# A new port rule in a kernel's scheduler, and its VectorE exponentials placed anew

## The chip, the cores and the metric

The kernel runs on one core of one Trainium2 chip. The metric is the device time of one execution in microseconds. A core has TensorE (PE, matrix products), ScalarE (ACT), VectorE (DVE), GpSimd (POOL) and SyncE (SP, which here only issues DMAs). Each engine runs its own instructions strictly in the order in which they were emitted, and waits for the others by semaphores.

## The reference

Two branches share one input of 2048 tokens by 640 features and are mixed by a gate. Branch A is a long convolution over the tokens, branch B is attention with 32 query heads of width 20 and one common key and value head.

```python
x = A_q
g = _sigmoid((x * gate_w).sum(-1, keepdims=True))
# A: short convolution of k (4 taps), times v, then a causal convolution of length 2048
kv = k_shift * v
y = irfft(rfft(pad(kv)) * rfft(pad(ssm_k)))[:S]
a = x * (y + kv * ssm_D)
# B: multi-query attention over all 2048 tokens, no mask
q, k, v = x @ wq, x @ wk, x @ wv
p = softmax(q k^T * 20 ** -0.5)
b = (p v) @ wo
out = g * a + (1 - g) * b
```

(The code is shortened; all inputs are bfloat16.) The exponentials of the softmax are the bulk: 32 x 2048 x 2048 of them.

## The kernel before

*The attention stream.* The work is cut into groups G of four heads by 512 queries, 32 in all (8 for each block of 512 queries). A group walks through 16 key blocks j of 128 keys. For each (G, j) there are four tiles, one for each head, of 128 keys by 512 queries. TensorE computes a tile's scores into a PSUM bank (`score`, L1205 in the profile), ScalarE takes the exponential (`EXP`, L1242), and TensorE multiplies the result with the values into the group's accumulator bank (`PVmm`, L1283). Tiles go to ScalarE in units of three and two by turns: a unit of three tiles is written to a buffer ETA (one instruction of 1536 columns), a unit of two to ETB (1024 columns). There are three buffers of each kind. PSUM banks 0 to 2 and 3 to 4 hold the scores of the A and the B unit, bank 6 is the accumulator, and banks 5 and 7 serve everything else. The last group is cut into three stages (`STAGES`), so that its end is short.

*Exponentials on VectorE.* The table `DVE_J` lists, for each group, the key blocks j of which two of the four tiles are not given to ScalarE. Such a (G, j) is called a pair here. `stream` takes the two tiles out of ScalarE's sequence and `DEXP` computes them: each tile's scores are made by a score matmul of their own in bank 5 or 7 (it "rides" beside the stream's score matmuls in other rows of the array), VectorE brings each to dW (L1272, 512 columns), and three `scalar_tensor_tensor` instructions on 1024 columns make the exponential (L1275, L1276, both writing dX, and L1278 writing ETd). The values' matmul of a pair is a floating one: it is put in when it is ready, and at the latest ahead of the group's last value matmul. There are two dW, one dX and four ETd.

*The end of a group.* `norm` copies the accumulator to SBUF (acc, VectorE, L1351), sends the denominators through DRAM by three DMAs (den, scr_d, rbc) with a reciprocal on VectorE between (L1356), and GpSimd multiplies (oTn or oT, L1363). A DMA carries the result to DRAM for the output projection of that block of queries (L1662 and L1665; for the last block part of it directly, L1388 and L1391).

*The convolution.* It runs beside the stream as spectral products: for five blocks of 128 channels, TensorE computes spectra of kv and of the filter (`spectra`, L1566), VectorE evicts them to X and K (L1579, L1585, L1587), GpSimd multiplies them (`mac`, L1599, tiles Pp and AB), and TensorE transforms back (`inverse`, L1632), with VectorE's eviction into kv (L1642). Its transform tables are made in the first 75 us, in part by GpSimd.

*What sets the order.* Nothing in the order is written out by hand. `build` makes a graph of operations with dependencies, priorities and an estimated cost each, and `Scheduler` simulates the five engines by these costs when the kernel is built. Whenever an engine is free in this plan, `pick` chooses an operation and `place` sets its start and end; the order in which operations are placed is the instruction order that `emit` writes out, together with the semaphore waits. A wrong cost thus changes no result, only the order. ScalarE's exponentials and TensorE's matmuls of the stream are a fixed main sequence; all else is fitted in around it. Where TensorE would be idle for long in the plan, filler matmuls that write nothing needed are put in (L1714).

*The port.* VectorE and GpSimd share a read port of SBUF. Operations that use it carry `port=True`: VectorE's three steps of a pair, the squares sq, table steps and a few more. In `place`, one variable `port_until` says until when the port is taken; a VectorE operation with the mark and every GpSimd operation begin no earlier than that and move it to their own end. `pool_may` further lets GpSimd start only when VectorE's last planned instruction doesn't use the port, or none is soon to.

Of the kernel before, what the change touches and what calls it, by code (L numbers as in the profile page):

```python
# [48 lines left out]
class Op:  # L49
# [4 lines left out]
    def __init__(self, eng, fn, cost, kind, name, prio):  # L54
        self.unit = None
        self.eng = eng
        self.fn = fn
        self.deps = set()
        self.cost = cost
        self.kind = kind  # L60
        self.name = name
        self.prio = prio
        self.grp = None
        self.alts = None
        self.port = False
        self.nbytes = 0
        self.main = False
        self.cont = False
        self.nun = 0
        self.succ = []  # L70
        self.ready = 0.0
        self.start = None
        self.end = None
        self.placed = False
        self.sig = False
        self.value = None
        self.lane = None
        self.known = None
        self.seq = -1
        self.banks = None  # L80
        self.last = False
        self.urge = False
        self.floating = False
        self.tail = ()
        self.attached = False
        self.lat = 2.2
        self.iss = 0.35
        self.row = None
        self.soft = ()
        self.cols = frozenset()  # L90
        self.hole = frozenset()
# [78 lines left out]
class Scheduler:  # L170


    def __init__(self, graph, bank_free=(0, 1, 2, 3, 4, 5, 6, 7)):
        self.g = graph
        self.order = {e: [] for e in ENGS}
        self.linear = []
        self.t = {e: BEGIN for e in ENGS}
        self.bank_ready = {b: 0.0 for b in range(8)}
        self.bank_last = {b: [] for b in range(8)}
        self.bank_busy = {b: False for b in range(8)}  # L180
        self.bank_claimed = {b: False for b in range(8)}
        self.port_until = 0.0
        self.dma_bw = 0.0
        self.lanes = [[] for _ in range(NLANES)]
        self.main_started = False
        self.filler = None
        self.acc = None
        self.can_fill = False
        self.filler0 = None
        self.float_left = []  # L190
        self.active = []
        self.rows = set()
        self.mode = "f"
# [255 lines left out]
    def place(self, op, e):  # L449
        t = self.t[e]  # L450
        op.eng = e
        if e == "pe":
            mode = MODE.get(op.name, "f")
            if mode != self.mode:
                t += SWITCH
                self.mode = mode
        if op.alts:
            for x in op.alts:
                self.cand[x].discard(op)
            op.fn, op.cost = op.alts[e]  # L460
        else:
            self.cand[e].discard(op)
        if op.main and e == "pe":
            for b in op.banks or ():
                if not self.bank_claimed[b]:
                    self.bank_claimed[b] = True
                    op.deps.update(self.bank_last[b])
        start = max(t, op.ready)
        if op.kind == "d":
            if op.nbytes:  # L470
                begin = max(start + 0.1, self.dma_bw)
                self.dma_bw = begin + op.nbytes / 300e3
                op.end = max(self.dma_bw, start + op.iss) + op.lat
            else:
                op.end = start + op.iss + op.lat
            self.t[e] = start + op.iss
            best = min(range(NLANES), key=lambda l: self.lanes[l][-1].end if self.lanes[l] else -1.0)
            op.lane = best
            if self.lanes[best]:
                op.deps.add(self.lanes[best][-1])  # L480
            self.lanes[best].append(op)
            op.value = 16 * len(self.lanes[best])
        else:
            if (op.port and e == "dve") or e == "pool":
                start2 = max(start, self.port_until)
                op.end = start2 + op.cost
                self.port_until = op.end
            else:
                op.end = start + op.cost
            self.t[e] = op.end  # L490
        op.start = start
        op.placed = True
        if e == "pe" and op.cost > 0.05:
            self.active.append((op.end - op.cost * 0.92, op.end))
        if e == "pe":
            if op.name != "qk":
                self.rows = set()
            elif op.cont:
                self.rows.add(op.row)
            else:  # L500
                self.rows = {op.row}
        if op.name in ("tp0", "tp1"):
            b = STAGES[int(op.name[2])][2]
            self.bank_claimed[b] = self.bank_busy[b] = False
            self.bank_last[b] = [op]
            self.bank_ready[b] = op.end + LATX
            self.filler = self.filler2.pop(0) if self.filler2 else None
        if op.name == "pv":
            self.can_fill = not op.last
            self.acc = None  # L510
        elif op.name == "acc":
            self.acc = op
        if e == "pool" and self.main_started and HOLD:
            d = self.order["dve"]
            if len(d) > 1 and d[-1].end > t and not d[-1].port:
                op.deps.add(d[-2])
        self.order[e].append(op)
        self.linear.append(op)
        gr = op.grp
        if gr is not None:  # L520
            if e == "pe" and op in gr.mms:
                gr.pos += 1
                if gr.pos == len(gr.mms) and self.open is gr:
                    self.open = None
            elif op in gr.evacs:
                if all(x.placed for x in gr.evacs):
                    b = gr.bank
                    self.bank_busy[b] = False
                    self.bank_last[b] = [gr.mms[-1]] + list(gr.evacs)
                    self.bank_ready[b] = max(x.end + (LATX if self.main_started else LATS[x.eng, "pe"]) for x in gr.evacs)  # L530
        for s in op.succ:
            s.nun -= 1
            lat = 0.0 if (s.eng == "pe" and e == "pe") else self.lat_of(op, e, s.eng)
            s.ready = max(s.ready, op.end + lat)
            sg = s.grp
            if sg is not None and s.eng == "pe" and not (op.grp is sg):
                sg.nun -= 1
                sg.ready = max(sg.ready, op.end + lat)
                if sg.nun == 0:
                    self.gcand.add(sg)  # L540
            if s.nun == 0:
                self.enable(s)
# [87 lines left out]
UP = 256.0  # L630

SIDE = (7, 5)
LASTG = 31
STAGES = ((0, 256, 6), (256, 128, 5), (384, 128, 6))
DVE_J = ((), (5,), (), (1, 6, 11), (2, 11), (3, 8, 13), (5, 13), (2, 9), (3, 6, 9, 12), (3, 9, 13), (4, 9, 14), (1, 6, 11), (4, 11), (2, 6, 10, 14), (2, 7, 12), (1, 8, 11), (3, 9), (2, 9, 12), (3, 8, 13), (1, 5, 9, 13), (2, 7, 12), (4, 8, 14), (3, 6, 13), (1, 4, 9, 13), (4, 11, 14), (3, 8, 13), (4, 9, 14), (3, 6, 9, 13), (1, 4, 7, 10, 13), (1, 4, 7, 9, 13), (2, 6, 12, 14), ())
MAC_ALT = ()
SCALE = float(DH) ** -0.5

# [25 lines left out]
class Kernel:  # L664
# [23 lines left out]

    def group(self, name, prio, banks=SIDE):
        gr = Group(banks, prio, name)  # L690
        self.g.groups.append(gr)
        return gr
# [466 lines left out]
    def stream(self):  # L1159
# [3 lines left out]
        order = (0, 1, 2, 3)  # L1163
        for G in range(LASTG + len(STAGES)):
            for j in range(NSC if G < LASTG else NSC * STAGES[G - LASTG][1] // 512):
                mine = order
                if G < LASTG and j in DVE_J[G]:
                    mine, rest = order[:2], order[2:]
# [11 lines left out]
    def attention(self):  # L1180
# [10 lines left out]
        def split(G):  # L1191
            return 512 // STAGES[G - LASTG][1] if G >= LASTG else 1

        def accb(G):
            return STAGES[G - LASTG][2] if G >= LASTG else 6

        def qkey(G):
            g = min(G, LASTG)
            return f"qT{g // 8 % 2}", g % 8
# [88 lines left out]
        def PV(G, j, rs, more=False):  # L1288
# [18 lines left out]
            if j == 0 and G < LASTG:  # L1307
                for jd in DVE_J[G]:
                    ek = ("ETd", self.ndexp % NED)
# [464 lines left out]
```

## Time and profile before

| | us |
|---|---|
| median of 3 runs | 874.34 |
| lowest, highest | 873.39, 874.41 |
| the profiled execution | 873.49 |
| its span, first to last instruction | 871.7 |
| ScalarE's first ETA starts | 20.16 |
| ScalarE's last ETA starts | 864.53 |
| idle time of VectorE in the span | 194.8 |

The profile is of one execution. The difference between the execution's time and its span lies before the first and behind the last instruction. A busy share is the time in which an engine executed something, whether useful or not; the granted TensorE clock was 1.0 throughout. Where an engine's records overlap, the mean duration of a record isn't the time that it takes from the engine, and the distance between starts has to be read instead. An instruction that shares the port has the waiting for it inside its recorded duration, not ahead of it.

### The profile page before, as it was taken

How to read it: one execution, taken by the hardware profiler on the slowest of the kernel's cores; microseconds unless marked ns; L12 is line 12 of the kernel's file. 1: busy time of each engine (PE TensorE's matmuls, PEld its weight loads, DVE VectorE, ACT ScalarE, POOL GpSimd, SP SyncE). 2: the span in 40 equal slices, each digit the busy share in tenths (PEclk: the TensorE clock that was granted, in tenths of full speed). 3: DMA queues.
4: the chain of work that ended last, by engine and by line, in shares of the span. 5: the costliest groups of instructions: out<-in, count | busy, mean ns of one | idle time of the engine just before them, and what ended most of it. 6: DMA issues, size and time to landing. Idle time of an engine off the chain costs nothing.

```text
span 871.7 us, 18992 instructions
## 1 busy us (share of the span) xinstructions
PE 851.6 (98%) x8223; PEld 351.9 (40%) x8223; DVE 676.9 (78%) x898; ACT 857.9 (98%) x768; POOL 361.3 (41%) x355
## 2 busy tenths in 40 slices
PE   8999999999999999999999999999999999999998
PEld 5234423443344334444333343443344443343334
DVE  7568988668868787677977867877877888898845
ACT  6999999999999999999999999999999999999997
POOL 4572001686614454653336433365443366400000
PEclk9999999999999999999999999999999999999999
DMA  6900010001000000100001120000100000221110
GB/s 194 211 14 9 20 46 20 14 14 35 22 22 16 17 9 19 44 20 14 20 10 31 32 58 14 19 8 20 45 21 20 14 2 14 55 70 37 59 66 33
DMA packets 49730, 30.72 MB, mean 35 GB/s; under 512 B 32493, under 2 KB 45678, under 8 KB 49646
## 3 DMA queue, kind: packets, MB, share of 16 engines
q1 hardware_dynamic: 49070, 29.29, 12.1%
q8 instruction: 64, 1.05, 0.5%
q10 hardware_dynamic: 576, 0.22, 0.1%
q14 instruction: 20, 0.16, 0.1%
HBM read 17.85 MB, written 6.02 MB: 27 GB/s over the span
## 4 chain that ended last, share of the span: by engine, by line
ACT 89%; PE 7%; DVE 3%; issue 0%; POOL 0%; POOLq 0%; DVEq 0%
ACT ETA L1242 53%; ACT ETB L1242 36%; PE ps L1566 2%; PE ps L1205 2%; PE ps L1283 1%; PE ps L1719 1%; DVE ETd L1278 1%; DVE dX L1276 1%; PE ps L1014 0%; DVE dW L1272 0%; DVE dX L1275 0%; PE ps L1046 0%; DVE X L1579 0%; PE ps L1388 0%; PE ps L1418 0%; PE ps L1714 0%
## 5 line engine op out<-in xcount | busy, mean ns | idle before, releaser
L1242 ACT ACTIVATE ETA<-ps 128x1536 bf16<-128x1536 f32 x374 | 608.2, 1626 | 1.1 <-PE ps L1205 0.9
L1242 ACT ACTIVATE ETB<-ps 128x1024 bf16<-128x1024 f32 x373 | 449.2, 1204 | 0.0
L1205 PE MATMUL ps<-qT,kT 32*128 32x512 bf16 (+2 forms) x2176 | 299.3, 371 | 12.5 <-ACT ETA L1242 5.5
L1599 POOL TENSOR_TENSOR Pp<-X,K 128x512 f32<-128x512 bf16 x120 | 148.6, 1257 | 151.7 <-DVE K L1587 58.3
L1205 PEld LDWEIGHTS ps<-qT,kT 32*128 32x128 bf16 x2176 | 75.7, 91 | 244.3 <-ACT ETB L1242 124.5
L1272 DVE TENSOR_SCALAR dW<-ps 128x512 f32<-128x512 f32 x180 | 123.4, 686 | 57.3 <-PE ps L1205 55.9
L1283 PE MATMUL ps<-ETA,vaug 128*32 128x512 bf16 (+2 forms) x1201 | 154.4, 370 | 0.0
L1283 PE MATMUL ps<-ETB,vaug 128*32 128x512 bf16 (+2 forms) x795 | 148.6, 371 | 0.1
L1278 DVE SCALAR_TENSOR_TENSOR ETd<-dX,dW 128x1024 int16<-128x1024 f32 x90 | 123.5, 1372 | 31.4 <-PE ps L1283 31.1
L1276 DVE SCALAR_TENSOR_TENSOR dX<-dX,dW 128x1024 f32<-128x1024 f32 x90 | 125.7, 1397 | 0.4
L1275 DVE SCALAR_TENSOR_TENSOR dX<-dW 128x1024 f32<-128x1024 uint16 x90 | 120.4, 1338 | 1.0
L1566 PE MATMUL ps<-ssm_kT,Tcs 128*128 128x256 bf16 x600 | 90.2, 275 | 0.4 <-DVE dW L1272 0.3
L1632 PE MATMUL ps<-AB,Tcs 128*128 128x256 bf16 x600 | 89.5, 274 | 0.3 <-DVE dW L1272 0.3
L1566 PE MATMUL ps<-kv,Tcs 128*128 128x256 bf16 x600 | 87.6, 275 | 0.0
L1363 POOL TENSOR_TENSOR oTn<-acc,rbc 128x512 bf16<-128x512 f32 x24 | 36.6, 1525 | 115.5 <-DMA rbc<-scr_d 35.2
L1599 POOL TENSOR_TENSOR AB<-Pp 128x256 bf16<-128x256 f32 x80 | 62.9, 787 | 50.5 <-DVE dX L1276 19.0
L1714 PE MATMUL ps<-Tcs,zeros 128*32 128x512 bf16 (+1 forms) x984 | 79.6, 383 | 0.1
L1599 POOL TENSOR_TENSOR Pp<-Pp 128x512 f32<-128x512 f32 x40 | 53.6, 1341 | 40.4 <-DVE dX L1275 24.2
L1632 PEld LDWEIGHTS ps<-AB,Tcs 128*128 128x128 bf16 x600 | 51.1, 98 | 33.7 <-issue 28.0
L1566 PEld LDWEIGHTS ps<-ssm_kT,Tcs 128*128 128x128 bf16 x600 | 50.4, 98 | 35.2 <-issue 26.9
L1566 PEld LDWEIGHTS ps<-kv,Tcs 128*128 128x128 bf16 x600 | 50.0, 97 | 34.9 <-issue 27.6
L1363 POOL TENSOR_TENSOR oT<-acc,rbc 128x512 bf16<-128x512 f32 x7 | 12.5, 1780 | 90.4 <-DMA rbc<-scr_d 87.9
(135 smaller groups left out, 651.0 us busy)
## 6 DMA issues: line engine op xcount, KB each, us to landing
rbc<-scr_d SPq DMA_DIRECT2D x31, 256.0 KB
scr_o<-oTn SPq DMA_DIRECT2D x24, 128.0 KB, 1.7
kv<-in_A_v_dram SPq DMA_DIRECT2D x4, 640.0 KB, 5.4
out_dram<-outsb SPq DMA_DIRECT2D x15, 160.0 KB, 1.9
xn<-in_A_q_dram SPq DMA_DIRECT2D x3, 640.0 KB, 7.2
oTp<-scr_o SPq DMA_DIRECT2D x12, 160.0 KB, 2.8
wog<-in_B_wo_dram SPq DMA_DIRECT2D x4, 200.0 KB
wo<-in_B_wo_dram SPq DMA_DIRECT2D x4, 200.0 KB, 3.3
```

The lines of the kernel that those rows point to most:

```text
L1205: return e.matmul(self.bank(bk, n, n * t), T["kT4"][32 * r:32 * r + 32, 128 * jt:128 * jt + 128], T[k][32 * r:32 * r + 32, g, q0:q0 + n], ...
L1242: op("act", lambda e: e.activation(et(n)[:, 0:w], self.ps[:, lo:lo + w], ACT.Exp, scale=SCALE), [("ps", base[n % 2] + k) for k in range(le ...
L1272: self.evac(gr, "dve", lambda e, bk, h=h: e.tensor_scalar(W[:, 512 * h:512 * h + 512], self.bank(bk), SCALE * LOG2E * 128.0, 128.0 * (127 ...
L1275: V(lambda e: e.scalar_tensor_tensor(X[:, :], w, DP, w, ALU.add, ALU.mult), [kW], ["dX"], c_ps(1024), **k)
L1276: V(lambda e: e.scalar_tensor_tensor(X[:, :], X[:, :], DQ, w, ALU.add, ALU.mult), [kW], ["dX"], c_ps(1024), **k)
L1278: V(lambda e: e.scalar_tensor_tensor(T[f"ETd{pe}"][:, :].bitcast(dt.int16), X[:, :], DA, W[:, :], ALU.mult, ALU.add), [kW, "dX"], [("ETd", ...
L1283: return op("pe", lambda e: e.matmul(self.bank(b, n)[32 * r:32 * r + 32, :], T[va][:, j, :], src, start=(j == 0), stop=(j == NSC - 1), til ...
L1363: self.pool(lambda e: e.tensor_tensor(out, T["acc"][:, :], T["rbc"][:, :], ALU.mult), ["acc", "rbc"], [key], c_pool(512), prio=p, port=Tru ...
L1566: self.mm(gr, lambda e, bk, lhs=lhs, rhs=rhs, comp=comp, n=n: e.matmul(self.bank(bk, 256, 256 * comp), lhs, rhs, start=(n == 0), stop=(n = ...
L1599: f = lambda e: e.tensor_tensor(out, a, b, alu)
L1632: self.mm(gr, lambda e, bk, lhs=lhs, fc=fc, comp=comp, h=h: e.matmul(self.bank(bk, 256, 256 * h), lhs, AB[:, fc, :, comp, :], start=(fc == ...
L1714: sch.filler, *sch.filler2 = ([[lambda e, r=r, st=st, b=b, n=n: e.matmul(self.bank(b, n)[32 * r:32 * r + 32, :], self.T["zeros"][:, 0:32], ...
```

## The change

The rule in `place` becomes two variables and two constants, and `DVE_J` is a new table.

```diff
         self.port_until = 0.0
+        self.pool_until = 0.0
...
-            if (op.port and e == "dve") or e == "pool":
-                start2 = max(start, self.port_until)
-                op.end = start2 + op.cost
+            if op.port and e == "dve":
+                op.end = max(start, self.pool_until - PORTP) + op.cost
                 self.port_until = op.end
+            elif e == "pool":
+                op.end = max(start, self.port_until - PORTD) + op.cost
+                self.pool_until = op.end
             else:
                 op.end = start + op.cost
...
+PORTP = 0.145
+PORTD = 0.04
...
-DVE_J = ((), (5,), (), (1, 6, 11), (2, 11), (3, 8, 13), (5, 13), (2, 9), (3, 6, 9, 12), (3, 9, 13), (4, 9, 14), (1, 6, 11), (4, 11), (2, 6, 10, 14), (2, 7, 12), (1, 8, 11), (3, 9), (2, 9, 12), (3, 8, 13), (1, 5, 9, 13), (2, 7, 12), (4, 8, 14), (3, 6, 13), (1, 4, 9, 13), (4, 11, 14), (3, 8, 13), (4, 9, 14), (3, 6, 9, 13), (1, 4, 7, 10, 13), (1, 4, 7, 9, 13), (2, 6, 12, 14), ())
+DVE_J = ((), (), (1, 6, 11), (4, 11), (2, 6, 10, 14), (4, 9, 14), (3, 8, 13), (3, 8, 11), (2, 6, 10, 14), (4, 9, 14), (1, 5, 8, 13), (2, 7, 12), (3, 8, 13), (2, 5, 8, 11, 14), (5, 12), (1, 5, 9, 13), (4, 9, 14), (4, 9, 14), (4, 9, 14), (1, 4, 8, 12), (2, 6, 10, 14), (3, 8, 13), (2, 4, 13), (1, 7, 13), (1, 6, 11), (1, 6, 11), (1, 4, 11), (3, 9), (1, 4, 7, 10, 13), (2, 5, 8, 11, 14), (2, 9), ())
```

In the plan, a VectorE operation on the port now begins at the earliest 0.145 us before GpSimd's last operation ends, and a GpSimd operation 0.04 us before VectorE's last port operation ends. The old table holds 90 pairs, the new one 95; 27 places are in both. No operation's code and no estimated cost is touched. Since the plan changes, the instruction order of every engine changes with it. Lines of the changed kernel from the scheduler's `place` on stand three and later five below the numbers used here.

## The prediction

> **What bounds the kernel now.** I read the page's busy line first, then its groups, then the instructions in order of time, then the waits, then busy time by stretch.
>
> The busy line and three groups (name, shapes, count | busy us, mean ns of one | idle us before them):
>
> ```profile
> PE 851.6 (98%) x8223; PEld 351.9 (40%) x8223; DVE 676.9 (78%) x898; ACT 857.9 (98%) x768; POOL 361.3 (41%) x355
> L1242 ACT ACTIVATE ETA<-ps 128x1536 bf16<-128x1536 f32 x374 | 608.2, 1626 | 1.1 <-PE ps L1205 0.9
> L1242 ACT ACTIVATE ETB<-ps 128x1024 bf16<-128x1024 f32 x373 | 449.2, 1204 | 0.0
> L1714 PE MATMUL ps<-Tcs,zeros 128*32 128x512 bf16 (+1 forms) x984 | 79.6, 383 | 0.1
> ```
>
> ScalarE and TensorE are both at 98%. TensorE's share contains 984 filler matmuls (79.6 us of record time, four at a time side by side) that compute nothing. ScalarE's contains none. Its 747 exponentials are the stream everything follows: 1.1 us idle. But 608.2 + 449.2 us is more than the 857.9 us that ScalarE was busy at all, so the records overlap, and a record's duration is not what an exponential costs. The cost is the distance from start to start (start us, duration, engine, instruction):
>
> ```profile
> 588.47 1.59 ACT L1242 ACTIVATE ETA<-ps 128x1536 bf16<-128x1536 f32 x1
> 589.80 1.18 ACT L1242 ACTIVATE ETB<-ps 128x1024 bf16<-128x1024 f32 x1
> 590.71 1.62 ACT L1242 ACTIVATE ETA<-ps 128x1536 bf16<-128x1536 f32 x1
> 592.03 1.21 ACT L1242 ACTIVATE ETB<-ps 128x1024 bf16<-128x1024 f32 x1
> 592.94 1.65 ACT L1242 ACTIVATE ETA<-ps 128x1536 bf16<-128x1536 f32 x1
> ```
>
> One round of an A and a B unit takes 2.24 us undisturbed (588.47 to 590.71), about 1.33 + 0.91. Over the run the first ETA starts at 20.16 and the last, the 374th, at 864.53: 844.37 us for 373 rounds, 2.264 each. The floor I read from clean stretches is 2.235. So 373 x 0.029 = 10.7 us of stall lie in the stream. About 8 us are a few hundredths nearly everywhere; 2.7 us are in five places: rounds of 2.50 and 2.73 at 361.3 and 363.8, 3.01 at 465.8, 2.39 and 2.41 at 563.5 and 570.4, 2.71 at 597.4, 2.64 at 674.5. The largest, in order of time:
>
> ```profile
> 463.01 1.27 POOL L1363 TENSOR_TENSOR oTn<-acc,rbc 128x512 bf16<-128x512 f32 x1
> 463.14 2.22 DVE L1278 SCALAR_TENSOR_TENSOR ETd<-dX,dW 128x1024 int16<-128x1024 f32 x1
> ...
> 465.28 0.68 DVE L1272 TENSOR_SCALAR dW<-ps 128x512 f32<-128x512 f32 x1
> 465.76 1.68 ACT L1242 ACTIVATE ETA<-ps 128x1536 bf16<-128x1536 f32 x1
> ...
> 466.02 0.39 PE L1205 MATMUL ps<-qT,kT 32*128 32x512 bf16 x1 [0.39 <-DVE dW L1272]
> ...
> 468.77 1.45 ACT L1242 ACTIVATE ETA<-ps 128x1536 bf16<-128x1536 f32 x1 [0.41 <-PE ps L1205]
> ```
>
> The reader is to see one chain: GpSimd's normalisation starts 0.13 us before VectorE's last step of a pair, which takes 2.22 us instead of 1.23; the next eviction of scores (dW) is a microsecond late; a score matmul of the following pair needs that bank, and TensorE executes in order, so the scores for ScalarE behind it are late; the round takes 3.01. Of the five places, those at 361, 466 and 597 have this form. That is how VectorE, never the bound by its share, costs time.
>
> Busy us in two stretches (PE, PEld, DVE, ACT, POOL):
>
> ```profile
> 75.00:100.00 25.00, 24.88 (x307) 12.06 (x310) 23.07 (x29) 25.00 (x24) 1.28 (x1) 1.00 0.06 18
> 575.00:600.00 25.00, 24.51 (x244) 9.60 (x247) 16.77 (x21) 25.00 (x23) 19.16 (x16) 1.00 0.06 18
> ```
>
> From 75 to 150 us GpSimd waits for spectra and VectorE has the port alone; afterwards both use it.
>
> **What the Trainium skill says.** "SBUF — State Buffer", Who interferes with whom: a VectorE instruction with two SBUF inputs and a GpSimd instruction that reads SBUF exclude each other, whoever issues first holds the pair, and the other blocks fully. The trace agrees and gives the size: of VectorE's port instructions, 88 are over 0.06 us too long, 42.7 us together, and in nearly all that I matched to one GpSimd instruction the end lies at that instruction's end, plus the usual 1.22 or 1.23 us, less 0.13 to 0.16 us. (463.01 + 1.27 + 1.23 - 0.15 = 465.36 = 463.14 + 2.22.) That subtraction is the new constant PORTP. "Perfetto Trace Analysis", Optimizing Scalar/DVE Operations, says that recorded latency runs beyond the busy time because the acknowledgement of writes overlaps the next instruction; the overlapping ETA records agree.
>
> **The change part by part.**
>
> *Pairs, 90 to 95.* Of the old places 27 stay, 63 go and 68 are new. Each pair takes two 512-wide tiles from ScalarE. Tiles on ScalarE before: 31 x 64 - 2 x 90 + 64 = 1868 = 374 x 3 + 373 x 2; after: 31 x 64 - 2 x 95 + 64 = 1858 = 372 x 3 + 371 x 2. The instruction order of the changed kernel has exactly these 372 and 371. Two rounds go: 2 x 2.264 = 4.5 us, all on the path, since ScalarE is the path from 20.16 to the end of its stream. (Record durations would claim 2 x (1.626 + 1.204) = 5.7 us; I reject that for the overlap.)
>
> *What VectorE gets.* A pair costs it two evictions of 0.60 and three steps of 1.14, start to start: 4.6 us, five pairs 23 us. It hides in 872 - 677 = 195 us of idle time. Whether it hides locally I checked by adding start-to-start durations along its new order between two copies of the accumulator, against the group's exponentials: before, groups 1 to 29 lie at 0.52 to 0.90; after, at 0.50 to 0.92, most between 0.7 and 0.88. The fullest is group 2, where GpSimd is idle. No group exceeds 1, so VectorE doesn't become the bound; where cover is gone a late pair costs what it did above, 0.2 to 0.8 us each.
>
> *What TensorE gets.* The same score and value matmuls (ten value matmuls move from ETA and ETB to ETd), and 888 fillers of 512 columns instead of 976, 32 of 128 instead of 8. The order spends 22 filler sets less, at 0.22 us each 4.8 us: room that the shorter stream takes. TensorE is tighter but not fuller of work.
>
> *Placement.* The first eight groups carry 18 pairs instead of 13, the last eight 23 instead of 27. VectorE and TensorE do convolution work later in exchange: the last spectrum matmul comes after 1,803 of 2,176 score matmuls instead of 1,715, some 34 us of stream at 844/2176 each. A stretch with 45 filler sets behind it is thereby used up (13 sets after). The inverse transform still ends at about the same point (1,945 against 1,935), the first projections start 35 score matmuls later, and the last partial projection comes 32 before the last score instead of behind it. So I cost this at nothing in the tail; if the cover failed, one projection's evictions (2 x 0.46) would lie bare.
>
> *The port rule.* It moves instructions, adds none: fewer microseconds are planned for each collision (0.145 when VectorE waits, 0.04 when GpSimd does). The old rule made VectorE late in the plan only, which left real slack behind each collision; the new one removes this slack. GpSimd's order changes by normalisations passing products; SP's by issues of den, scr_d, rbc and qT passing each other and the ssm_kT loads (1.5 us of issue in the plan). Nothing in SP's queue is on the path, as its results feed GpSimd and VectorE. In the head one table step moves ahead of an xT eviction on ScalarE, up to 0.5 us there; the start at 20.16 hangs on TensorE's chain, so I take 0, with 0.3 either way. The end behind the last exponential (871.7 - 864.53 = 7.2 us) keeps its order; 0.2 either way.
>
> *Stalls.* The trace can't show the new ones. Below: the five places vanish, as all hang on pairs or normalisations that move, -2.7. Above: twice as many, and the small waits grow by a quarter, +2.7 + 2.0. I take zero: more pairs and less slack against a rule that fits.
>
> *Sum.* The profiled execution took 873.49 (span 871.7 and 1.8 around it): 873.49 - 4.5 = 869.0. The median of the runs, 874.34, stands 0.85 above it; the forecast as a median is 869.8.
>
> **The rivals.**
> - *The collisions go too* (15%): stalls -2.7, 867.1. For it: the old rule misjudged each of the 88. Against: the large stalls start with a normalisation released by a DMA, whose landing no port rule knows.
> - *Most of it is given back* (13%): stalls rise by 3 to 6 us from VectorE groups at 0.75 to 0.88 that stood at 0.6 to 0.75: 873 to 876, around 873.5.
> - *Slower* (12%): late evictions of dW hold the in-order TensorE, at every normalisation. Each costs up to 0.8 us (the 3.01 round). It decides from 6.3 us on, eight such rounds more than now, with 31 normalisations to meet; at ten, 8 us, 877.8. For it: 95 chains and no planned slack. Against: VectorE's 55.9 us of waiting for scores now, where TensorE and not VectorE is late.
> - That the exponentials don't fall is excluded by the order.
>
> **How the numbers follow.** The forecast, two rounds less with stalls as now, has 60%: 869.8, own range 867.7 to 872. Around 874.34, 0.2% (1.75 us, about what a measurement of this kernel tells from no change) makes faster below 872.6 and slower above 876.1. Faster 0.60 + 0.15 = 0.75, within 0.13, slower 0.12. The range runs from 866.8 (the five places gone, head in favour) to 874.0, leaving out the upper half of the given-back case and the slower one.
>
> **What would show it.** 372 ETA and 371 ETB; last ETA near 860.0; mean round 2.26; DVE busy near 700; POOL unchanged. Rounds of 2.35 and more number about twelve as now, the longest beside normalisations. A mean round above 2.28, or ScalarE waiting on L1205 by many us, makes it wrong; below 2.255 the first rival is right. A first ETA off by more than 0.3 puts the head in it.

## The result and the profile after

| | before | after |
|---|---|---|
| median of 6 runs, us | 873.94 | 867.51 |
| lowest to highest | 873.39 to 874.41 | 867.0 to 868.7 |
| profiled execution | 873.49 | 867.0 |
| its span | 871.7 | 865.2 |
| first ETA starts | 20.16 | 19.55 |
| rounds from the first ETA to the last, mean | 373, 2.2637 | 371, 2.2604 |
| behind the start of the last ETA | 7.17 | 7.03 |

The ratio of the times is 0.9928, with 0.9916 to 0.9941 as its interval: the changed kernel is 0.7% faster. The spans of the two profiled executions differ by 6.5 us, and the last three rows say where: the start gives 0.61, the stream from the first ETA to the last 5.75 (844.37 to 838.62), the end 0.14.

The busy line and three groups of the page, as they were shown of the kernel before (name, shapes, count | busy us, mean ns of one | idle us before them):

```profile
PE 842.1 (97%) x8139; PEld 350.5 (41%) x8159; DVE 710.2 (82%) x923; ACT 852.8 (99%) x764; POOL 389.8 (45%) x355
L1247 ACT ACTIVATE ETA<-ps 128x1536 bf16<-128x1536 f32 x372 | 607.2, 1632 | 0.2 <-PE ps L1210 0.2
L1247 ACT ACTIVATE ETB<-ps 128x1024 bf16<-128x1024 f32 x371 | 449.5, 1212 | 0.0
L1719 PE MATMUL ps<-Tcs,zeros 128*32 128x512 bf16 (+1 forms) x920 | 74.2, 379 | 0.9 <-DVE acc L1356 0.7
```

372 and 371 exponentials stand where 374 and 373 stood, and ScalarE's records leave 0.2 us idle ahead of them in the whole stream. There are fewer fillers. VectorE's busy time grew by 33 us, GpSimd's by 29, though GpSimd executes the same 355 instructions. Its largest group shows why; first the line of the kernel before, from its groups, then that of the changed kernel:

```profile
L1599 POOL TENSOR_TENSOR Pp<-X,K 128x512 f32<-128x512 bf16 x120 | 148.6, 1257 | 151.7 <-DVE K L1587 58.3 <-DVE dX L1276 30.7 <-DVE dX L1275 26.4
```

```profile
L1604 POOL TENSOR_TENSOR Pp<-X,K 128x512 f32<-128x512 bf16 x120 | 164.7, 1390 | 156.5 <-DVE dX L1281 58.0 <-DVE dX L1280 31.9 <-DVE AB L1620 20.2
```

The same 120 products took 1390 ns each instead of 1257, in part because waits for the port lie inside the record. The same is to be seen at VectorE: of its port instructions 113 are now over 0.06 us too long, 55.5 us together, where 88 were, with 42.7 us. There is more contention than before, and it costs less.

Busy us in the two stretches shown of before (PE, PEld, DVE, ACT, POOL):

```profile
75.00:100.00 25.00, 24.75 (x293) 11.38 (x292) 22.81 (x34) 25.00 (x25) 3.77 (x5) 1.00 0.06 19
575.00:600.00 25.00, 24.72 (x248) 10.30 (x245) 21.72 (x27) 25.00 (x23) 15.26 (x11) 1.00 0.05 17
```

In both ScalarE is busy throughout, although VectorE is at 22.8 and 21.7 us of 25, in the second stretch 5 us more than before.

Stalls. Above the floor of 2.235 us a round the stream held 10.7 us before and holds 9.4 now. The rounds of 2.35 and more were 12 with 3.5 us above the floor, and are 15 with 2.4. The largest round is now 2.53 us, where it was 3.01. In order of time (start us, duration):

```profile
812.82 1.63 ACT L1247 ACTIVATE ETA<-ps 128x1536 bf16<-128x1536 f32 x1
...
813.48 1.12 PE L1667 MATMUL ps<-wo,oTp 128*128 128x320 bf16 x7
...
814.54 0.39 PE L1288 MATMUL ps<-ETd,vneg 128*32 128x512 bf16 x2
814.86 0.39 PE L1210 MATMUL ps<-qT,kT 32*128 32x512 bf16 x3
...
815.35 1.45 ACT L1247 ACTIVATE ETA<-ps 128x1536 bf16<-128x1536 f32 x1
```

No collision is in it, and GpSimd does nothing from 812 to 816 us. TensorE has seven projection matmuls and a pair's value matmuls ahead of the next three scores, which start 0.3 us too late. The chains of a normalisation and a late dW that made the large rounds before have gone from the head of the list.

The end, from the chain of waits:

```profile
858.40 1.35 ACT ETA L1247
...
859.79 0.43 PE ps L1288 x16
...
861.51 0.46 PE ps L1423 x2
...
861.99 0.88 DVE outsb L1478
```

Behind the last exponential comes nothing but the last group's own values, normalisation and projection. All work of the convolution was done before; the experiments show what that is worth.

### The start

The 0.61 us at the start lie in TensorE's warm-up, whose filler matmuls are the same in number in both kernels. One tile's instructions in the first 10 us with their durations (minimum, median, maximum in ns), of before and of the changed kernel:

```profile
L1719 PE MATMUL ps<-ident,zeros x16: 379/619/631, 2.7 to 9.0; 128*128 128x512 bf16 x16
```

```profile
L1724 PE MATMUL ps<-ident,zeros x16: 379/380/634, 2.7 to 7.8; 128*128 128x512 bf16 x16
```

In each execution these matmuls take about 0.62 us at first and 0.38 later, and when they switch differs: the changed kernel's profiled execution had most of them at the short duration. The first experiment, whose scheduler is the changed one, had most of them at the long one (a median of 634 ns) and started its stream at 20.35. Over the 14 profiled executions of this study the first ETA starts between 19.55 and 21.23.

The trace also holds the granted TensorE clock, and its first record, of the full clock, begins where the matmuls become short. (Ahead of it there is no record, so a mean granted clock of 1.0 leaves this time out.) Six of the fourteen, in us:

| | first record of the full clock | first ETA starts |
|---|---|---|
| changed kernel | 5.41 | 19.55 |
| experiment 8 | 5.66 | 19.67 |
| before | 6.64 | 20.16 |
| experiment 1 | 7.04 | 20.35 |
| experiment 3 | 8.19 | 20.92 |
| experiment 5 | 8.70 | 21.23 |

A line fitted through all fourteen (16.87 us plus 0.496 of the switch) misses none by more than 0.05 us, although the order ahead of the stream is not the same in all of them. Experiment 1 has the changed kernel's order there, on TensorE, VectorE, ScalarE and GpSimd, and starts 0.8 us later. So the start follows the switch of the clock, and the order of the head shows in none of these starts. The 0.61 us belong to one execution and not to the change.

### The profile page after: what moved, and what is told of

Its sections match the earlier page's. It is cut to its first block, busy times and chain, and to the rows that moved or that the text cites. A ratio compares the mean times of both kernels' runs of the same rounds, so it can differ in the third digit from the quotient of the medians.

```text
span 865.2 us, 18881 instructions
## 1 busy us (share of the span) xinstructions
PE 842.1 (97%) x8139; PEld 350.5 (41%) x8159; DVE 710.2 (82%) x923; ACT 852.8 (99%) x764; POOL 389.8 (45%) x355
## 4 chain that ended last, share of the span: by engine, by line
ACT 97%; PE 2%; DVE 0%; issue 0%; POOL 0%; POOLq 0%
ACT ETA L1247 58%; ACT ETB L1247 39%; PE ps L1724 1%; PE ps L1019 0%; PE ps L1051 0%; ACT xT L726 0%; PE ps L1115 0%; DVE outsb L1478 0%; DVE tprod L912 0%; POOL iota_f L865 0%; PE ps L1210 0%; PE ps L1423 0%; PE ps L1288 0%; DVE ident L873 0%; DVE acc L1409 0%
## 5 line engine op out<-in xcount | busy, mean ns | idle before, releaser
L1604 POOL TENSOR_TENSOR Pp<-X,K 128x512 f32<-128x512 bf16 x120 | 164.7, 1390 | 156.5 <-DVE dX L1281 58.0
L1277 DVE TENSOR_SCALAR dW<-ps 128x512 f32<-128x512 f32 x190 | 130.2, 685 | 42.6 <-PE ps L1210 40.7
L1283 DVE SCALAR_TENSOR_TENSOR ETd<-dX,dW 128x1024 int16<-128x1024 f32 x95 | 134.2, 1413 | 15.4 <-PE ps L1288 15.2
L1281 DVE SCALAR_TENSOR_TENSOR dX<-dX,dW 128x1024 f32<-128x1024 f32 x95 | 133.6, 1407 | 0.2
L1280 DVE SCALAR_TENSOR_TENSOR dX<-dW 128x1024 f32<-128x1024 uint16 x95 | 131.5, 1385 | 0.9
L1604 POOL TENSOR_TENSOR AB<-Pp 128x256 bf16<-128x256 f32 x80 | 73.4, 917 | 57.7 <-DVE dX L1280 21.3
L1368 POOL TENSOR_TENSOR oTn<-acc,rbc 128x512 bf16<-128x512 f32 x24 | 41.2, 1716 | 84.4 <-DMA rbc<-scr_d 37.7
L1719 PE MATMUL ps<-Tcs,zeros 128*32 128x512 bf16 (+1 forms) x920 | 74.2, 379 | 0.9 <-DVE acc L1356 0.7
L1604 POOL TENSOR_TENSOR Pp<-Pp 128x512 f32<-128x512 f32 x40 | 52.7, 1317 | 34.9 <-DVE dX L1281 10.8
L1368 POOL TENSOR_TENSOR oT<-acc,rbc 128x512 bf16<-128x512 f32 x7 | 10.7, 1524 | 80.0 <-DMA rbc<-scr_d 47.8
```

What stands on the lines that cost most here:

```text
L1277: self.evac(gr, "dve", lambda e, bk, h=h: e.tensor_scalar(W[:, 512 * h:512 * h + 512], self.bank(bk), SCALE * LOG2E * 128.0, 128.0 * (127 ...
L1280: V(lambda e: e.scalar_tensor_tensor(X[:, :], w, DP, w, ALU.add, ALU.mult), [kW], ["dX"], c_ps(1024), **k)
L1281: V(lambda e: e.scalar_tensor_tensor(X[:, :], X[:, :], DQ, w, ALU.add, ALU.mult), [kW], ["dX"], c_ps(1024), **k)
L1283: V(lambda e: e.scalar_tensor_tensor(T[f"ETd{pe}"][:, :].bitcast(dt.int16), X[:, :], DA, W[:, :], ALU.mult, ALU.add), [kW, "dX"], [("ETd", ...
L1368: self.pool(lambda e: e.tensor_tensor(out, T["acc"][:, :], T["rbc"][:, :], ALU.mult), ["acc", "rbc"], [key], c_pool(512), prio=p, port=Tru ...
L1604: f = lambda e: e.tensor_tensor(out, a, b, alu)
```

## The experiments

Each kernel was compared with runs of the kernel before on the same chip (medians 873.5 to 873.9). All of them compute the whole of the reference. The figures in the table after the median are from each one's profile: when the first ETA starts, the stall above 2.235 us a round, and the time from the start of the last ETA to the end. "Last inverse" is after how many of the 2,176 score matmuls the convolution's last inverse-transform matmul stands in TensorE's order.

| kernel | pairs, rule | median us | ratio, interval | start | stall | end | last inverse |
|---|---|---|---|---|---|---|---|
| before | 90, old | 873.94 | | 20.16 | 10.7 | 7.17 | 1,935 |
| after | 95, new | 867.51 | 0.9928 (0.9916 to 0.9941) | 19.55 | 9.4 | 7.03 | 1,945 |
| 1 | 90 (old table), new | 873.65 | 1.0003 (0.9995 to 1.0011) | 20.35 | 9.9 | 7.02 | 1,924 |
| 2 | 95 (new table), old | 887.9 | 1.0167 (1.0154 to 1.018) | 21.06 | 13.1 | 23.12 | 2,084 |
| 3 | new table, old rule in the head | 870.21 | 0.9964 (0.9951 to 0.9977) | 20.92 | 10.3 | 8.56 | 1,955 |
| 4 | old table, new rule in the head | 882.18 | 1.0104 (1.0086 to 1.0123) | 20.64 | 18.0 | 11.52 | 1,973 |
| 5 | new table, PORTP 0.140 | 872.98 | 1.0 (0.999 to 1.0011) | 21.23 | 14.1 | 9.54 | 1,963 |
| 6 | new table, rule too fast | 888.08 | 1.016 (1.0145 to 1.0175) | 21.02 | 29.2 | 6.93 | 1,935 |
| 7 | five pairs fewer, new | 880.43 | 1.0079 (1.0067 to 1.0091) | 21.05 | 10.5 | 13.74 | 1,975 |
| 8 | five pairs more, new | 879.7 | 1.0075 (1.0063 to 1.0087) | 19.67 | 18.5 | 14.63 | 1,980 |
| 9 | 94 searched, old | 870.03 | 0.9964 (0.995 to 0.9978) | 20.24 | 10.6 | 7.91 | 1,914 |
| 10 | the same 94, new | 878.52 | 1.0057 (1.0044 to 1.0069) | 20.76 | 16.4 | 10.31 | 1,955 |
| 11 | 97 searched, new | 868.39 | 0.994 (0.9926 to 0.9953) | 20.93 | 10.6 | 7.65 | 1,954 |
| 12 | 98 searched, new | 866.7 | 0.9922 (0.9908 to 0.9935) | 20.45 | 10.8 | 6.70 | 1,951 |

The last two columns belong together. In the seven kernels whose last inverse comes after 1,954 score matmuls or earlier, the end takes 6.70 to 7.91 us; in the seven with 1,955 and more it takes 8.56 to 23.12. Start, stall and end are of one execution each. Executions of the kernel before differ by 1.0 us and those of the changed kernel by 1.7, so differences of about 1 us in these columns may be of the execution.

### 1 and 2: each half of the change alone

Experiment 1 is the changed kernel with the old table, experiment 2 the kernel before with the new table:

```diff
@@ experiment 1, from the changed kernel
-DVE_J = ((), (), (1, 6, 11), (4, 11), ...
+DVE_J = ((), (5,), (), (1, 6, 11), (2, 11), ...
@@ experiment 2, from the kernel before
-DVE_J = ((), (5,), (), (1, 6, 11), (2, 11), ...
+DVE_J = ((), (), (1, 6, 11), (4, 11), ...
```

> The old table of 90 pairs, planned with the new port rule. If the gain is the two rounds that the five pairs take from ScalarE, nothing large comes back here: 374 ETA and 373 ETB, mean round 2.26, time within 1.5 us of before's 873.9. If the rule itself makes the order better, the stalls fall: mean round 2.255 or less, time 871 or less. If the rule alone harms the old table (less slack behind each collision), mean round over 2.27 and 876 or more.

> The new table of 95 pairs, planned with the old rule. If the pairs carry the gain by themselves: 372 ETA and 371 ETB, two rounds or 4.5 us less than before, about 869.4, at most 1.5 us above the changed kernel. If the pairs need the rule they were placed with: mean round 2.27 to 2.28, 870.5 to 874.

The rule alone is worth nothing (1.0003), as the first theory had it. The table alone, which contains the two rounds, is 14 us slower than the kernel before, and neither theory had that. (Its mean round, 2.270, is what the second theory named, but most of the time is lost elsewhere.) So the halves don't add up: 0 and +14 make -6.4 together. ScalarE has the 372 and 371 exponentials in experiment 2 too. What happened is in the chain of waits of experiment 2 at its end:

```profile
864.07 1.06 PE ps L1662 x7
...
865.46 5.29 PE ps L1662 x35
870.75 2.46 PE ps L1388 x18
...
873.23 0.56 DVE part L1391
...
883.33 0.88 DVE outsb L1473
```

Behind the last scores TensorE still has 35 matmuls of the output projection (L1662) and then all the partial projections of the last block (L1388), with VectorE's evictions of them. In the changed kernel the last partial projection stands ahead of the last 32 scores. With the old rule the same table puts the last inverse transform after 2,084 scores, not 1,945, and the projections, which need its result, fall out of the stream: an end of 23.1 us instead of 7.0. Of the 21.3 us between the two profiled spans (886.5 and 865.2) the end makes 16.1, stalls 3.7 and the start 1.5.

### 3 and 4: the rule in the head only

In experiment 3 the changed kernel plans by the old rule until the stream begins and by the new one from there on. Experiment 4 is the reverse, with the old table: the new rule in the head and the old one behind it.

```diff
@@ in place, ahead of the new branches
+            if not self.main_started and ((op.port and e == "dve") or e == "pool"):
+                op.end = max(start, self.port_until, self.pool_until) + op.cost
+                self.port_until = self.pool_until = op.end
+            elif op.port and e == "dve":
-            if op.port and e == "dve":
```

Experiment 4 has `self.main_started` without the `not`, and the old table.

> The changed kernel, with the old rule until the first exponential is placed, so that VectorE and ScalarE have before's order ahead of the stream. The profile of the changed kernel starts the stream at 19.55, that of before at 20.16. If the order in the head made this, the stream starts at 20.1 to 20.2 here and the time is 0.6 us above the changed kernel. If it is the speed of the 15 warm-up matmuls, which went from 619 to 380 ns a microsecond earlier in that execution, the start lies anywhere from 19.5 to 20.2 and has nothing to do with the rule; the time then differs by the rest of the stream's order only, within 1 us.

> The kernel before, with the new rule in the head only, so that VectorE and ScalarE have the changed kernel's order ahead of the stream. If the order in the head is worth 0.6 us: stream starts at 19.5 to 19.6, time 873.3. If it is the warm-up: a start anywhere from 19.5 to 20.2, time within 1 us of before. ETA and ETB as before, 374 and 373.

Experiment 3 lost 2.7 us against the changed kernel by the medians; in its profile the end is 1.5 us longer, the stalls 0.9, and the start, 20.92, lies where its clock's switch at 8.19 puts it. Neither theory had it in this form. Experiment 4 fits neither either, with 8.7 us lost to the kernel before: rounds of 4.64 and 4.09 us at 172 to 177 us, one of 4.42 at 363.8, and an end longer by 4.4. (Its runs spread from 879.7 to 885.6 us, with the granted clock, of which more at the end: the profile is of the slowest of them, and those rounds lie around two of its three stretches at half the clock.) A handful of instructions in the first 20 us, placed by another rule, changes where things meet 150 us and 800 us later. What was to be read from it, the price of the head, can't be read from its time; the starts above give it.

### 5 and 6: the constants of the rule

```diff
@@ experiment 5
-PORTP = 0.145
+PORTP = 0.14
@@ experiment 6
-PORTP = 0.145
-PORTD = 0.04
+PORTP = 0.6
+PORTD = 0.4
```

> The changed kernel with 0.140 in place of 0.145. As a statement about the port the two can't be told apart, but the order changes throughout: the last inverse matmul comes after 1,963 score matmuls instead of 1,945, and the partial projections reach to the last score matmul instead of ending 32 ahead. If the rule's truth makes the gain, any true rule has it: 867 to 868. If the table is fitted to one plan, a part is lost: 1 to 2 us more tail behind the last exponential (8 to 9 us, changed kernel 7.0), 868.5 to 870, rounds still near 2.26.

> The changed kernel with 0.6 and 0.4 in place of 0.145 and 0.04: the plan lets VectorE and GpSimd overlap more than they do, some 0.45 us for each of about 90 collisions. The convolution stands early in the order (last inverse after 1,935 score matmuls, last partial projection after 2,064), so the tail should be 7.0. If only the convolution's end matters, 867 to 868. If the plan must not promise what the port doesn't give, late evictions hold TensorE: stalls in the stream 15 to 25 us instead of 9.4, 873 to 883.

Five nanoseconds off the constant cost 5.5 us by the medians. About 4.6 of them are the order's: the six runs with the full clock throughout took 871.9 to 872.4 us, and the other eight have a lower mean clock (shown at the end). The theory that a table fits one plan had foretold a loss with an end of 8 to 9 us, and 9.5 came, but it did not have the stalls; of the 14.1 us in the profile, a run with the slower clock, 4.5 lie in the four rounds around that stretch. No port behaves differently by that; the plan does. Its last inverse moved from 1,945 to 1,963 and the end grew by 2.5 us, and two rounds in the stream fell late (shown at the end). The table of 95 pairs is fitted to one plan and loses with this one as with the old rule's (experiment 2).

Experiment 6 bears out the theory that the rule must not promise too much, and beyond its numbers: here such a rule does the opposite of the old one in experiment 2. The convolution is in time (last inverse 1,935, end 6.93), but 49 rounds take 2.35 us or more and the stalls make 29.2 us, 20 us more than in the changed kernel. TensorE waits 5.6 us for evictions to dW in it, where the list of the changed kernel's waits has none, and 7.5 us for qT, X and K. About 9 of the 29.2 us lie in five rounds around stretches at half the clock. In this pair of runs, then, the rule's error has two prices: the plan that is too slow puts work behind the stream, the one that is too fast puts scores behind late evictions. Busy us in experiment 6 (PE, PEld, DVE, ACT, POOL, granted clock) hold one such place:

```profile
55.00:66.00 11.00, 10.83 (x120) 4.87 (x121) 9.76 (x12) 11.00 (x12) 10.54 (x9) 1.00 0.08 27
66.00:70.00 4.00, 2.12 (x19) 0.48 (x11) 2.06 (x3) 3.93 (x4) 3.12 (x5) 0.98 0.04 13
70.00:75.50 5.50, 5.34 (x39) 1.97 (x39) 3.68 (x6) 1.99 (x2) 2.61 (x4) 0.50 0.05 17
```

In the second line TensorE has half its time idle, waiting for VectorE's qT (2.04 us), which VectorE brought late because a table step ahead of it waited 2.59 us for GpSimd. In the third line ScalarE has 2 us of work in 5.5, at half the clock.

### 7 and 8: five pairs fewer, five more

```diff
@@ experiment 7, group: its row of the table now
+ 4: (2, 6, 10)   8: (2, 6, 10)   13: (2, 5, 8, 11)   28: (1, 4, 10, 13)   29: (2, 5, 11, 14)
@@ experiment 8
+ 14: (2, 7, 12)  22: (2, 4, 9, 13)  25: (1, 6, 11, 14)  27: (3, 9, 13)  30: (2, 6, 10)
```

> The changed kernel with five of its 95 pairs given back to ScalarE, in groups 4, 8, 13, 28 and 29. Two rounds more, 374 ETA and 373 ETB. If rounds are what is paid for: stream 4.5 us longer than the changed kernel's, 872 with the same tail, up to 874 if the tail grows (partial projections reach to the last score matmul here). If VectorE's density cost stalls, the stream is longer by less than 4 us because mean rounds fall below 2.255.

> The changed kernel with five more pairs, 100, in the emptier groups 14, 22, 25, 27 and 30. 370 ETA and 369 ETB. If rounds pay without limit: 863. If the convolution's end is the limit: stream 4.5 us shorter, but the last inverse comes after 1,980 score matmuls and the partial projections reach to the last, tail 9 to 12 instead of 7.0: 865 to 868. If VectorE is the limit: mean round above 2.27 and no gain.

Both are 6 to 7 us slower than the kernel before, further than any theory with a number had them, and neither tells the price of a pair. The mean round of experiment 8, 2.285, is above the 2.27 that was to mark a VectorE at its limit, but one round makes it; the other 368 take 2.263 on average. Experiment 7 has stalls of 10.5 and lost 6.7 us at the end, experiment 8 lost 7.6 there and 8 us in a single round of 10.6 us. In order of time:

```profile
801.95 1.45 ACT L1247 ACTIVATE ETA<-ps 128x1536 bf16<-128x1536 f32 x1
...
804.50 1.80 PE L1637 MATMUL ps<-AB,Tcs 128*128 128x256 bf16 x15
...
806.11 1.23 DVE L1281 SCALAR_TENSOR_TENSOR dX<-dX,dW 128x1024 f32<-128x1024 f32 x1
...
807.87 0.39 PE L1210 MATMUL ps<-qT,kT 32*128 32x512 bf16 x1
...
808.59 0.68 DVE L1277 TENSOR_SCALAR dW<-ps 128x512 f32<-128x512 f32 x1
808.73 1.53 PE L1667 MATMUL ps<-wo,oTp 128*128 128x320 bf16 x10 [0.47 <-DVE kv L1647]
809.18 1.22 DVE L1283 SCALAR_TENSOR_TENSOR ETd<-dX,dW 128x1024 int16<-128x1024 f32 x1
...
811.62 1.02 ACT L1247 ACTIVATE ETB<-ps 128x1024 bf16<-128x1024 f32 x1 [8.22 <-PE ps L1210]
```

ScalarE waits 8.22 us for scores while TensorE executes inverse transforms and projections. They stand ahead of the last value matmuls of group 29, which need ETd of its pair (29, 14). That pair is in the changed kernel's table too; none of the five added ones is in this group. VectorE's step for ETd starts 1.8 us after the step before it has ended, since VectorE's order has an eviction to kv and a dW of the next pair ahead of it, and this dW needs a score matmul (807.87) that stands behind some thirty matmuls of the inverse transform. GpSimd does nothing here (0.00 us busy from 801.9 to 812.5), so no collision made it: the order that the plan made with the five pairs puts ETd where it comes late.

### 9 to 12: tables searched on the plan

The tables were found by a local search on the plan alone, that is, pairs were shifted or added and a table was kept when the planned end came earlier. Experiment 9 is the kernel before with such a table of 94; 10 is the same table with the new rule; 11 and 12 are the changed kernel with tables of 97 and 98.

```diff
@@ experiments 9 and 10, groups 1 to 8 of 31
+DVE_J = ((), (13,), (11,), (1, 3, 8, 11), (2, 7), (2, 9, 11), (6, 14), (2, 6, 8), (1, 3, 8, 13), ...
@@ experiment 12
+DVE_J = ((), (), (1, 6, 12), (4, 11), (3, 8, 11, 14), (5, 9, 14), (3, 11, 13), (2, 8, 12), (2, 6, 10, 13), ...
```

> The kernel before with its old rule and another table: 94 pairs, found by a local search that starts from the old table and shortens the plan made with the old rule. 1,860 tiles on ScalarE, 372 ETA and 372 ETB, 0.9 us of stream more than the changed kernel. The convolution ends early (last inverse after 1,914 score matmuls). If a table only has to be fitted to its own plan, the old rule does nearly as well as the new one: 868 to 869.5. If the rule has to be true, the stream stalls or the tail grows: 872 or more.

> The same table of 94 pairs planned with the new rule. If the truth of the rule makes good orders out of any table: as the run with the old rule or better, 867.5 to 868.5. If a table serves the plan it was fitted to: tail or stalls grow by 5 us and more (last inverse after 1,955 score matmuls instead of 1,914, partial projections to the last score matmul), 874 to 880.

> The changed kernel with a table of 97 pairs, fitted by a local search to the plan with the new rule. 1,854 tiles on ScalarE, 4 fewer, 1.8 us of stream. If fit and count make the time: 865.7, with tail near 7 and stalls near 9. If the changed kernel was at the limit of VectorE: mean round 2.27 or more, no faster than 867.5.

> The changed kernel with a table of 98 pairs, fitted in the same way. 1,852 tiles, 6 fewer, 2.7 us of stream. If fit and count make the time: 864.8. If VectorE is at its limit: mean round 2.27 or more, and no faster than the run with 97.

Experiment 9 gains 3.6 us of 873.6 without any new rule, between the values that the two theories had for it. Experiment 10 gives it back and 4.9 us more, as the theory of a fit had it, with rounds of 5.92 and 5.53 us: a table that is good under one rule is bad under the other, in both directions (2 and 10). The old table of 90 is no worse under the new rule (1), so not every table is fitted so closely. Experiments 11 and 12 take two and three pairs more than the change did and get to 868.4 and 866.7. Both were expected lower, at 865.7 and 864.8 if fit and count make the time. The other theory, a VectorE at its limit, is right on 11 in that it is no faster than 867.5, but its mark, a mean round of 2.27, is in neither (2.264), and 12 is faster than 11. The interval of 12 overlaps that of the changed kernel, so it is not shown to be better. It has a round less than the changed kernel, and 1.4 us more of stalls (10.8). One round of 4.16 us at 757, with a stretch at half the clock in it, makes 1.9 of them.

## Why the prediction was right, and where it wasn't

The forecast for the profiled execution was 869.0, and 867.0 came. The missing 2.0 us are stalls (1.2), the start (0.6) and the end (0.1). The likeliest case, two rounds less, was the one that came, but it is the counts and the mean round that say so and not the time. The median of 867.51 lies just under that case's own range (867.7 to 872), 2.3 us from its 869.8 and 0.4 from the first rival's 867.1. Luck has a part in how far it went: 0.6 us of the profiled difference is an early switch of the clock.

- *Two rounds off ScalarE*, 4.5 us: right, counts and size. 5.75 us went from the stream, of which two rounds at 2.264 are 4.53.
- *Stalls kept*, with -2.7 to +4.7 as bounds: mis-sized at zero. 371 rounds at 2.2604 instead of 2.2637 are 1.2 us less. This is one execution of each kernel, so it stays open how much of the 1.2 the change made. The large rounds account for 1.1 of it (3.5 to 2.4 us above the floor), the small waits for almost nothing. The first rival's mark, a mean round below 2.255, was not reached, and its reason doesn't hold either: the overlong port instructions, 88 before, are 113.
- *"The new one removes this slack"*, by which I held more stalls possible: not borne out. With the new rule alone (experiment 1) the stalls are 9.9 and not more than the 10.7 before. A rule that promises too much has 29.2 (experiment 6), but experiments 4, 8 and 10 have 16 to 19 too, so the rule isn't all that sets them.
- *VectorE hidden*: right. It is busy 710 us and not 700, since the waits inside its records grew by 12.8 us, and no ScalarE time went with it.
- *Placement at nothing in the tail*: right for the changed kernel (7.03), but my price for the lost cover, "one projection's evictions (2 x 0.46)", was wrong by far. Experiment 2 lost 16 us there, 7 and 8 some 7 each. The term isn't one eviction, it is every projection that the last inverse transform holds back. None of my rivals had this mechanism; the slower one had late dW alone, which experiment 6 shows, with late qT, X and K beside it.
- *The head, 0.3 either way*: 0.61 came, and my mark would have put it down to the head's order. The start moves with the switch of the clock, by 1.7 us over fourteen executions, so the mark could not tell.
- *"POOL unchanged"*: wrong by 29 us of busy time, as I forgot that its records hold its waits; it bought and cost nothing.

The median of before was 874.34 in the three runs that I started from and 873.94 in the six of the result; 0.4 us of the distance from 869.8 to 867.51 are that.

What is not settled: how much of the changed kernel's lead of 2.5 us over experiment 9 is owed to the rule and how much to the search that found the table. The two have one table each, and both of these tables lose under the other rule. Whether the new constants are the port's true law isn't shown by times at all, as five nanoseconds move the plan as much as a wrong law does. That the old rule delays the convolution in experiment 2 *because* it charges each collision too much is read from the code and the orders, not measured alone.

## What to carry to other kernels

Where a simulated plan sets the instruction order, a cost model and a table fitted to its plan are one change, to be tried together and against a table refitted for the old model; here the new table tried alone measured the misfit. Before the stream's rate is looked at, find in the order where the last work that does not belong to the stream stands, and what is behind it: here an end that came out cost up to 16 us and a round 2.26. Look at which way a model errs: in the one run of each kind, too slow put work behind the stream and too fast put waits into it. The converse doesn't hold, as experiments 7, 8 and 10 have long ends, and 8 and 10 long rounds too, under the new rule.

## What I had not expected of the hardware

A short idle of TensorE inside a busy stream was followed by a longer stretch at half the clock. In experiment 5, and below it in experiment 12, busy us (PE, PEld, DVE, ACT, POOL, granted clock):

```profile
237.39:240.80 3.41, 2.16 (x19) 0.59 (x16) 3.41 (x4) 3.26 (x4) 0.05 (x1) 1.00 0.00 0
240.80:247.63 6.83, 6.66 (x37) 2.18 (x37) 4.12 (x8) 3.78 (x3) 2.72 (x3) 0.50 0.03 5
247.63:251.04 3.41, 3.41 (x33) 1.21 (x31) 2.81 (x4) 3.01 (x4) 0.00 (x0) 1.00 0.21 76
```

```profile
754.67:758.08 3.41, 1.88 (x23) 0.47 (x20) 3.41 (x5) 3.41 (x4) 2.25 (x2) 1.00 0.00 0
758.08:761.49 3.41, 3.41 (x30) 0.81 (x28) 3.35 (x5) 1.88 (x3) 3.19 (x3) 0.50 0.06 10
```

Three lines of experiment 5 in order of time:

```profile
240.97 0.62 PE L1719 MATMUL ps<-Tcs,zeros 128*32 128x512 bf16 x4 [1.34 <-DVE acc L1356]
241.52 0.61 PE L1210 MATMUL ps<-qT,kT 32*128 32x512 bf16 x3
...
249.56 0.39 PE L1210 MATMUL ps<-qT,kT 32*128 32x512 bf16 x2
```

TensorE was idle for 1.25 of the 3.41 us before 240.80, nearly all in the one piece of 1.34 us in which it waited for the copy of an accumulator, and which ends at 240.97. From 240.80 its clock stood at 0.50 for 6.83 us, a score matmul took 0.61 us instead of 0.39, and rounds took 3.96 and 4.09 us. Experiment 5's fourteen runs fall apart by their mean granted clock: six at 1.0 took 871.9 to 872.4 us, three at 0.998 took 872.9 to 873.3, five at 0.996 took 875.5 to 875.9. So the same order meets this in some executions only, and then pays some 3.5 us. (6.83 us at half the clock are 0.004 of 874, and one stretch of 3.41 would be 0.002.) Experiment 6 shows the same above, after a wait of 2.04 us, and twice more, and experiment 4 three times, among them after 1.80 us for a dW at 173 us and after 1.31 us for a DMA (ssm_kT) at 364.6.

The fourteen traces together say more. Inside the streams there are eight such stretches, three each in experiments 4 and 6 and one in 5 and 12. Each lasts 3.41 or 6.83 us and begins a whole multiple of 3.41 us after the trace's first record of the full clock (68 times 3.413 us in experiment 5, 220 times in 12). I therefore cut every stream into pieces of 3.413 us from that record on and added up TensorE's idle time, by its records, in each. The pieces just ahead of the eight stretches hold 1.15 to 1.75 us of it, in experiment 12 in waits of at most 0.95. No other piece inside a stream holds more than 1.19. (A piece with 1.15 was followed by half the clock and the one with 1.19 was not, so the limit is not sharp in these records, in which the ends of matmuls are modelled.) What counted here was thus the idle time within one such piece, with a limit near 1.2 us, and not the length of one wait. That one order meets it only sometimes fits this, since the first record lies anywhere from 5.41 to 8.70 us and a wait can be split between two pieces; only one execution of each is traced, so this part is not shown. Nor did a run change the idle time alone. Behind the streams the limit doesn't hold: pieces with up to 1.88 us of idle kept the full clock there, and why is open.

The Trainium skill, "TensorE: Matmul & The Clock Gate", What's actually happening, has the half clock after at least one idle window of about 3.4 us. Here about half of such a window and less was enough, so a wait of TensorE of 1.3 us came to cost some 3.5. The fillers are there to keep TensorE busy, but they are placed by the plan, and these waits were not in it.
